# Block-sparse attention with an FFN: transposes of P into the free score columns, six early buffers for P, and more buffers for its halves

## The chip, the cores and the metric

The kernel runs on one core of a Trainium2 chip. The metric is the device time of one execution in microseconds (us), the median of several runs.

Engines are named as the profile names them: PE is TensorE's matmuls, PEld its weight loads, DVE is VectorE, ACT is ScalarE, POOL is GpSimd, SP is SyncE, which here only issues transfers. Each engine runs its own instructions in order and waits for other engines through semaphores.

## The reference

Attention over 4 batches of 8 heads, 768 positions, 64 wide, with a mask over blocks of 32: a block sees its neighbours, the first and last blocks, and three sampled ones. Behind it a layer norm, a feed-forward network (FFN) with a ReLU, 512 to 2048 to 512, and a residual.

```python
scores = scale * np.matmul(q, k.transpose(0, 1, 3, 2))
...
scores = np.where(mask, scores, -1000000000.0)
scores = scores - np.max(scores, axis=-1, keepdims=True)
attn = np.exp(scores)
attn = attn / (np.sum(attn, axis=-1, keepdims=True) + 1e-09)
x = np.matmul(attn, v)           # then (B, S, 8 * 64)
...
xn = (x - mu) / np.sqrt(var + 1e-06) * g_ln
out = x + np.maximum(xn @ w_ch1, 0.0) @ w_ch2
```

## The kernel before

Numbers that go into a matmul are split into a high and a low half in f16, and a product is the sum of three: high by high, high by low, low by high. In tile names `kh`, `kl` are the halves of k, `qh`, `ql` of q, `ph`, `pl` of P, `xh`, `xl` of the normed rows, `hh`, `hl` of the hidden layer, `w1h`, `w1l`, `w2h`, `w2l` of the weights. The weights come in a wide integer form and are unpacked on DVE (lines 514 to 564) out of the raw tiles `w1r` and `raw`.

The work is cut into 12 units of 256 rows (of one batch), each with 4 pairs of heads: 48 segments. A segment has two tiles of 128 rows by two heads: 4 slots, 192 in all. Scores are made for two slots at a time, a pair: slots 2n and 2n+1 are pair n. Each of the two slots has a score tile `ps` in PSUM, 128 partitions by 1024 floats, of which the scores fill columns 0 to 767; a PSUM bank holds 512 floats of each partition, so a score tile spans two banks. The chain for a slot is: scores on PE (L587) into `ps`; masked max on DVE (L596) from `ps` and the mask table `allow` into `p`, with the maximum in `st` (the tile `st2n` is that of pair n); the exponential on ACT (L610), in place in `p`.

After that there are two ways. The first 9 segments (EARLY, 36 slots) go through PE: P is transposed in f32, four of its six 128-column tiles into one PSUM bank and the other two into another (L625; three tiles `bank`, 512 floats each, shared with the FFN and the layer norm), ACT copies both out into `pt` (L632), PE multiplies with v (L701), spreads the sums over partitions (L726), and DVE scales (L733). The other segments make `ph` on ACT (L662) and `pl` on DVE (L666), transpose both by DMA from SP's queue (L672, L675), and multiply with v (L705, L710). The raw keys lie in two buffers `raw0`, `raw1` of 2 x 768 floats, of which the loads use the first 768.

After four segments a unit is complete; it gets its layer norm, then the FFN (L302). The first unit's FFN is placed among the scores of later segments. DVE builds the mask table in two parts: one for the first 256 rows, and one for the rest (L314 to L319), with an integer table in `w1h`'s place.

The order on every engine is made by a planner when the program is built (class `Plan`). Tasks have an engine, a cost in ns, a rank, the tasks that they follow, and resources that they take and give back: rings, whose places go round, and choices, in which the place that came free first is taken. At each step the planner takes the task that can start first by its own costs and emits its instructions. It also puts filler matmuls (ones by ones) into early gaps of PE. The numbers near the head of the function set ranks and choices: MASKAT is the rank of the second part of the mask table, EASE the slack that a task is planned with (PE below rank 44, PE above, other engines above), EXPO and EVAC shift the ranks of exponentials and copies, KDVE and QDVE say how many low halves of k and q DVE makes rather than POOL, CASTK and CASTQ how many high halves ACT casts rather than POOL's DMA. Real waits are semaphores that the framework sets from the tiles and banks that instructions touch, not from the planner's costs.

Of the kernel before, what the change touches and what calls it, by code (L numbers as in the profile page):

```python
# [10 lines left out]
F16 = mybir.dt.float16  # L11
F32 = mybir.dt.float32
# [164 lines left out]
def sparse_attention_moe(  # L177
# [12 lines left out]
    nc = tc.nc  # L190
    P = 128
    B, NPAIR, NCH, _, CH = qs.shape
    D = P // 2
    S = ks.shape[3]
# [10 lines left out]
    NQ = 4  # L205
    UPS = H * TS

    EARLY = 9
    EARLYLN = 1
    EASY, EASE = 44, (249, 2530, 951)  # L210
    PORC = ((2, 0), (2, 7), (1, 1), (2, 11), (2, 9), (1, 6), (2, 13), (2, 10), (1, 4), (2, 1), (2, 2))
# [3 lines left out]
    SPLITAT = 7.38  # L215
    VDVE = 1
    KDVE, QDVE = 3, 1
    HIDMA = ((1, 5), (2, 15), (2, 2), (1, 7), (2, 5), (2, 4))
    LEAD = 2.8
    HIGHAT, LOWAT = -0.42, -1.36  # L220
    EVAC, EXPO = -9.12, 1.22
    PLAIN = 'full'
    LOWDVE = ((2, 12), (1, 3), (2, 2), (1, 6), (1, 1), (2, 8), (2, 11), (1, 7), (2, 4), (2, 15), (2, 6), (2, 3), (1, 0), (2, 13), (2, 5))
    AVHOLD = 4
    KEEP = 40000.0
    CASTK, CASTQ = 5, 6
    MASKAT = 25.07
    KAT, VAT, QAT = 11.39, 7.48, 12.65
    AVAT = -17.05
    W1AT = (8.87, 9.4, 10.72, 12.06, 12.3, 15.45, 16.92, 18.19)  # L230
    W2AT = (10.6, 14.04, 14.21, 15.7, 17.12, 20.44, 21.31, 22.16, 23.71, 24.25, 25.32, 25.67, 25.7, 25.75, 26.19, 28.74)
# [5 lines left out]
    pp = ctx.enter_context(tc.tile_pool(name="pp", bufs=2))  # L237
# [6 lines left out]
    ps_s = ctx.enter_context(tc.tile_pool(name="ps_s", bufs=2, space=bass.MemoryType.PSUM))  # L244
# [4 lines left out]

    plan = Plan()  # L250
# [33 lines left out]
    ql_s = [const.tile([P, CH], F16, name=f"ql{i}") for i in range(NQ)]  # L284
    w1h = const.tile([P, CT, DF], F16, name="w1h")
# [54 lines left out]
    def loads_k(b, pr, rank, before):  # L340
        idx = b * NPAIR + pr
        o = SimpleNamespace()

        def raw():
# [3 lines left out]
            nc.sync.dma_start(o.kr, ks[b, pr])  # L348
# [4 lines left out]
        o.raw = plan.add("SP", 580, raw, (before,), rank, 2000, load=1120, order="k",  # L353
# [5 lines left out]
        else:  # L359
            o.high = plan.add("POOL", 560, lambda: nc.gpsimd.dma_start(o.kh, ks[b, pr]),  # L360
                              (o.raw,), rank, 2300, load=1100, order="k")
# [4 lines left out]
    def loads_q(n, rank, before):  # L366
        u, pr = segs[n].u, segs[n].pr
        o = SimpleNamespace()

        def raw():  # L370
# [4 lines left out]
            nc.sync.dma_start(o.qr, qs[u.b, pr, u.c])  # L375

        o.raw = plan.add("SP", 580, raw, (before,), rank, 2000, load=370, order="q",
# [5 lines left out]
        else:  # L383
            o.high = plan.add("POOL", 560, lambda: nc.gpsimd.dma_start(o.qh, qs[u.b, pr, u.c]),  # L384
                              (o.raw,), rank, 2300, load=400, order="q")
# [47 lines left out]
    def loads_v(b, pr, rank, before):  # L433

        o = SimpleNamespace(idx=b * NPAIR + pr, vr={}, raw=[])
        early = any(x.early for x in segs if (x.u.b, x.pr) == (b, pr))
# [11 lines left out]
        for j in range(2):  # L448
            def raw(j=j):
# [6 lines left out]
                nc.sync.dma_start(dst.rearrange("p t d -> p (t d)"), v[b, 2 * pr + j])  # L456

            take = (() if early else (("vr", (o.idx, j)),)) + ((("v", o.idx),) if j == 0 else ())
            o.last = plan.add("SP", 580, raw, (o.last,), rank, 2000, load=550, take=take, order="v")
# [8 lines left out]
    def loads_w(kind, i, before, w1done, low_tail):  # L468

        o = SimpleNamespace()  # L470
        own = (kind, i)
        if kind == 1:
# [11 lines left out]
        def load():  # L484
# [18 lines left out]
            nc.sync.dma_start(o.raw.rearrange("p e t -> p (e t)"),  # L503
# [33 lines left out]
        ld = plan.add("SP", 580, load, after if kind == 1 or i >= 10 else after + tuple(  # L537
# [29 lines left out]
        if own in HIDMA and own in PORC:  # L567
            o.high = plan.add("POOL", 560, lambda: nc.gpsimd.dma_start(o.dh, o.src), (d,), rank + HIGHAT,
                              2300, load=1500 * size)
# [20 lines left out]
    def masked_max(s):  # L590
        s.p = pp.tile([P, S], F32, tag="p", name=f"p{s.i}", bufs=4)
# [21 lines left out]
    def attention_early(seg, pair, e_done):  # L613
        r = pair[0].i
        for s in pair:
            key = (seg.i, s.h % 2)
            x4 = x2 = None
            for part, (lo, hi) in enumerate(((0, 4), (4, KT))):
# [3 lines left out]
                def turn(s=s, lo=lo, hi=hi, own=own):  # L622
                    dst = bank[plan.where("bank", own)]
# [4 lines left out]
                def out_(s=s, lo=lo, hi=hi, own=own, dve=dve, key=key):  # L628
                    if key not in pts:
                        pts[key] = ptp.tile([P, KT, CH], F32, tag="pt", name=f"pt{key[0]}_{key[1]}")  # L630
                    src = bank[plan.where("bank", own)][:, 0 : (hi - lo) * P]
# [4 lines left out]
                             take=(("bank", own),), give=(("p", s.i),) if part else ())  # L636
                take = (("pt", key),) if s.t == 0 and part == 0 else ()
                y = plan.add("DVE" if dve else "ACT", 335 if dve else (470, 300)[part], out_,
                             (x,) if part == 0 else (x, seg.first[key]) if s.t == 0 else (x,),
                             r + EVAC, 130, take=take, give=(("bank", own),))  # L640
# [4 lines left out]

    def attention(seg, pair, e_done):
        r = pair[0].i

# [7 lines left out]
        for s in pair:  # L656
            key = (seg.i, s.h % 2)

            def high(s=s):
                s.ph = pp.tile([P, S], F16, tag="ph", name=f"ph{s.i}")  # L660
# [3 lines left out]
            def low(s=s):  # L664
                s.pl = pp.tile([P, S], F16, tag="pl", name=f"pl{s.i}")
# [11 lines left out]
            h = plan.add("ACT", 830, high, (inv,), r, 120, take=(("ph", s.i, 2),))  # L677
# [449 lines left out]
```

## Time and profile before

| | |
|---|---|
| time, median of 3 runs | 794.59 us (793.11 to 795.34) |
| the profiled execution | 792.63 us, its span 790.9 us |
| instructions on PE, DVE, ACT, POOL | 7327, 1216, 935, 140 |
| costliest group of matmuls | 204.6 us, the FFN's second layer, high by high |
| masked maxima on DVE | 192, 178.1 us, 950 ns each |
| exponentials on ACT | 192, 178.4 us, 931 ns each |
| `pl` on DVE | 156, 160.1 us, 1040 ns each |

The span is the time from the first to the last instruction of one profiled execution; that execution's own time lies 1.7 us above it. Busy times are sums over an engine's instructions. A row of the timeline has an instruction's start, its length, engine, line, what it writes and reads, and in brackets the idle time before it with what ended it. A row of the waits has the waiting engine and line, what it waited for, the total, how often, and the longest.

### The profile page before, as it was taken

To read this page: it belongs to the slowest core of one execution; us is meant where nothing else is said; L and a number is where in the kernel's file an instruction comes from. 1 tells how busy PE (TensorE), PEld (TensorE's weight loads), DVE (VectorE), ACT (ScalarE), POOL (GpSimd) and SP (SyncE) were. 2 spreads that over 40 slices of the span, in tenths; PEclk is the share of its full clock that TensorE was granted. 3 is DMA by queue.
4 is the path that set the end of the run, shared out by engine and by line. 5 is a ranking of instruction groups with operands and counts; after the bars stand their busy time and mean duration, and the time that the engine had idled before them with its cause. 6 is when DMAs were issued, how large, how long until landed. Compare 5 with 4: busy or idle time off the path is not lost.

```text
span 790.9 us, 18452 instructions
## 1 busy us (share of the span) xinstructions
PE 777.9 (98%) x7327; PEld 599.3 (76%) x7327; DVE 615.4 (78%) x1216; ACT 498.3 (63%) x935; POOL 130.4 (16%) x140
## 2 busy tenths in 40 slices
PE   8999999999999999999999999999999999999998
PEld 5556677778777777777777777777777877778887
DVE  7999999979888778879877978778877878874220
ACT  6789776567676566667666667567656656652110
POOL 1343542321101002220101102120001100000000
PEclk9999999999999999999999999999999999999999
DMA  9463537998777567999667778997866755570000
GB/s 331 163 194 118 152 106 152 199 213 162 166 129 135 126 129 146 188 196 155 159 123 127 135 137 150 186 190 161 160 105 125 154 115 114 123 136 18 21 1 27
DMA packets 286694, 111.24 MB, mean 141 GB/s; under 512 B 253968, under 2 KB 278416, under 8 KB 286608
## 3 DMA queue, kind: packets, MB, share of 16 engines
q1 hardware_dynamic: 278544, 104.91, 61.2%
q0 software_dynamic: 7776, 5.05, 5.5%
q8 instruction: 57, 0.93, 0.5%
q14 instruction: 29, 0.24, 0.1%
q10 hardware_dynamic: 288, 0.10, 0.1%
HBM read 47.16 MB, written 6.29 MB: 68 GB/s over the span
## 4 chain that ended last, share of the span: by engine, by line
PE 88%; DVE 5%; ACT 3%; DMA 3%; issue 0%; ACTq 0%; DVEq 0%
PE bank L302 61%; PE ps L587 12%; PE pa L705 7%; PE pa L710 3%; PE pa L701 2%; PE bank L625 2%; DMA pt<-pl 2%; DVE p L596 1%; ACT p L610 1%; ACT pt L632 1%; DVE pl L666 1%; DVE allow L317 0%; DMA allow<-blocks 0%; PE pa L726 0%; PE bank L782 0%
## 5 line engine op out<-in xcount | busy, mean ns | idle before, releaser
L302 PE MATMUL bank<-hh,w2h 128*128 128x256 f16 x768 | 204.6, 273 | 0.0
L302 PE MATMUL bank<-hh,w2l 128*128 128x256 f16 x768 | 204.2, 273 | 0.0
L302 PE MATMUL bank<-hl,w2h 128*128 128x256 f16 x768 | 204.2, 273 | 0.0
L596 DVE CUSTOM_DVE_ANT_1 p<-ps,allow 128x768 f32<-128x768 f32 x192 | 178.1, 950 | 22.9 <-PE ps L587 22.6
L610 ACT ACTIVATE p<-p,st 128x768 f32<-128x768 f32 x192 | 178.4, 931 | 18.5 <-DVE st L596 18.2
L662 ACT ACTIVATE ph<-p,st 128x768 f16<-128x768 f32 x156 | 140.4, 927 | 59.6 <-DVE st L653 20.7
L666 DVE SCALAR_TENSOR_TENSOR pl<-p,st,ph 128x768 f16<-128x768 f32 x156 | 160.1, 1040 | 10.5 <-DMA pt<-pl 10.5
L302 PEld LDWEIGHTS <-w2h 128*128 128x128 f16 x1536 | 146.7, 98 | 27.0 <-issue 10.5
L302 PEld LDWEIGHTS <-w1h 128*128 128x128 f16 x1536 | 147.8, 98 | 25.5 <-issue 8.8
L302 PE MATMUL bank<-xh,w1h 128*128 128x256 f16 x768 | 115.4, 273 | 1.0 <-ACT pt L632 1.0
L302 PE MATMUL bank<-xh,w1l 128*128 128x256 f16 x768 | 115.4, 273 | 0.0
L302 PE MATMUL bank<-xl,w1h 128*128 128x256 f16 x768 | 115.4, 273 | 0.0
L889 DVE SCALAR_TENSOR_TENSOR hl<-bank,hh 128x512 f16<-128x512 f32 x96 | 66.1, 688 | 53.9 <-ACT hh L883 53.2
L883 ACT ACTIVATE hh<-bank 128x512 f16<-128x512 f32 x96 | 56.8, 591 | 75.3 <-PE bank L302 74.7
L302 PEld LDWEIGHTS <-w1l 128*128 128x128 f16 x768 | 73.8, 98 | 12.4 <-issue 4.1
L302 PEld LDWEIGHTS <-w2l 128*128 128x128 f16 x768 | 75.0, 98 | 9.1 <-issue 0.3
L705 PE MATMUL pa<-pt,vh 128*64 128x512 f16 x468 | 80.0, 383 | 0.9 <-DMA pt<-pl 0.9
L384 POOL DMA_DIRECT2D qh<-q x42 | 24.3, 579 | 277.7 <-PE ps L587 277.6
L587 PE MATMUL ps<-kh,qh 64*128 64x256 f16 (+1 forms) x384 | 66.0, 328 | 1.2 <-DVE st L596 1.1
L387 POOL TENSOR_TENSOR ql<-qr,qh 128x256 f16<-128x256 f32 x47 | 43.9, 935 | 139.9 <-DMA qr<-q 77.3
L587 PE MATMUL ps<-kl,qh 64*128 64x256 f16 (+1 forms) x384 | 64.4, 323 | 1.6 <-DVE kl L351 1.6
L587 PEld LDWEIGHTS <-qh 64*128 64x128 f16 x768 | 30.9, 94 | 45.8 <-issue 23.5
(110 smaller groups left out, 906.7 us busy)
## 6 DMA issues: line engine op xcount, KB each, us to landing
qr<-q SPq DMA_DIRECT2D x48, 128.0 KB, 2.8
raw<-k SPq DMA_DIRECT2D x16, 384.0 KB, 4.6
raw<-w SPq DMA_DIRECT2D x12, 512.0 KB, 3.9
vr<-v SPq DMA_DIRECT2D x32, 192.0 KB, 2.8
out<-ot SPq DMA_DIRECT2D x48, 128.0 KB, 1.9
w2l<-w SPq DMA_DIRECT2D x4, 1024.0 KB, 8.1
qh<-q POOLq DMA_DIRECT2D x42, 64.0 KB, 2.8
pt<-ph SPq DMA_TRANSPOSE x156, 2.7
```

The source lines that it names most:

```text
L302: nc.tensor.matmul(dst, w, x, start=start, stop=stop, skip_group_check=True)
L384: o.high = plan.add("POOL", 560, lambda: nc.gpsimd.dma_start(o.qh, qs[u.b, pr, u.c]), (o.raw,), rank, 2300, load=400, order="q")
L387: o.low = plan.add(e, x, lambda: (nc.vector if n < QDVE else nc.gpsimd).tensor_sub(o.ql, o.qr, o.qh), (o.raw, o.high), rank, give=(("qr", ...
L587: nc.tensor.matmul(s.ps[:, lo:hi], x[rows, s.qs], y[rows, lo:hi], start=n == 0, stop=n == len(terms) - 1)
L596: nc.vector.tensor_tensor_reduce(out=s.p.rearrange(blk, k=BLK), in0=s.ps[:, 0:S].rearrange(blk, k=BLK), in1=bias, scale=-0.125, scalar=3.0 ...
L610: nc.scalar.activation(s.p, s.p, AF.Exp, bias=s.st[:, j : j + 1], scale=-1.0, accum_out=total)
L662: nc.scalar.activation(s.ph, s.p, AF.Copy, scale=s.r)
L666: nc.vector.scalar_tensor_tensor(out=s.pl, in0=s.p, scalar=s.r, in1=s.ph, op0=ALU.mult, op1=ALU.subtract)
L705: nc.tensor.matmul(seg.pa[half[hh], 0 : 2 * CH], vo.vh[:, hh, t, :], pts[keys[hh]][:, t].rearrange("p i n -> p (i n)"), start=t == 0, stop ...
L710: nc.tensor.matmul(seg.pa[half[hh], 0:CH], vo.vl[:, hh, t, :], pts[keys[hh]][:, t, 0, :], start=False, stop=t == KT - 1, skip_group_check= ...
L883: nc.scalar.activation(u.hh[:, f : f + 2, :].rearrange("p f n -> p (f n)"), bank[plan.where("bank", own)], AF.Relu)
L889: nc.vector.scalar_tensor_tensor(out=u.hl[:, f : f + 2, :].rearrange("p f n -> p (f n)"), in0=bank[plan.where("bank", own)], scalar=0.0, i ...
```

## The change

The score tiles become two fixed tiles. The last two transposes of an early slot, and ACT's copy of them, use columns 768 to 1023 of a score tile rather than a `bank`; the planner has a choice "rest" of two places for these columns, apart from the ring "ps" of the score tiles. P gets six places for the early segments: four tiles, and two more that are the later halves' tiles, seen as f32. The halves get four places each: the two old ones and, from segment WIDEAT = 14 on, two in the second 768 floats of `raw0` and `raw1`. A helper `queue_of` can put loads on POOL's queue; with `POOLQ = ()` every one stays on SP's. A few planned costs and all numbers at the head of the function are changed; some are shown. The other numbers set the ranks of loads, weights and casts in the same way.

```diff
-    EASY, EASE = 44, (249, 2530, 951)
+    EASY, EASE = 44, (85, 2233, 956)
-    KDVE, QDVE = 3, 1
+    KDVE, QDVE = 12, 0
-    EVAC, EXPO = -9.12, 1.22
+    EVAC, EXPO = -16.38, 8.36
-    CASTK, CASTQ = 5, 6
-    MASKAT = 25.07
+    CASTK, CASTQ = 6, 16
+    MASKAT = 22.15
...
+    plan.choice("p", range(6))
+    plan.choice("rest", range(2))
+    plan.choice("ph", range(4))
+    plan.choice("pl", range(4))
...
+    score = [ps_s.tile([P, 1024], F32, tag=f"ps{i}", name=f"ps{i}") for i in range(2)]
...
+    p_s = [const.tile([P, S], F32, name=f"p{i}") for i in range(4)]
+    halves_s = [const.tile([P, 2, S], F16, name=f"p{n}") for n in "hl"]
+    p_s += [x.rearrange("p i s -> p (i s)").bitcast(F32) for x in halves_s]
...
-            s.ps = ps_s.tile([P, 1024], F32, tag="ps", name=f"ps{s.i}")
+            s.ps = score[plan.where("ps", s.i)]
...
-        s.p = pp.tile([P, S], F32, tag="p", name=f"p{s.i}", bufs=4)
+        s.p = p_s[plan.where("p", s.i)]
...
-                    dst = bank[plan.where("bank", own)]
+                    dst = score[plan.where("rest", own)][:, S:] if part else bank[
+                        plan.where("bank", own)]
...
-                    src = bank[plan.where("bank", own)][:, 0 : (hi - lo) * P]
+                    src = score[plan.where("rest", own)][:, S:] if part else bank[
+                        plan.where("bank", own)]
...
                 x = plan.add("PE", 110 * (hi - lo), turn, (e_done[s.i], x4), r, 230, mode="full",
-                             take=(("bank", own),), give=(("p", s.i),) if part else ())
+                             take=((("bank", "rest")[part], own),), give=(("p", s.i),) if part else ())
                 take = (("pt", key),) if s.t == 0 and part == 0 else ()
+                if part and seg.i < EARLY - 2:
+                    wides.append(x)
...
+    def half_of(n, place):
+
+        if place < 2:
+            return halves_s[n][:, place]
+        return raw_s[place - 2][:, S:].bitcast(F16)[:, n * S : (n + 1) * S]
...
+        late = seg.i >= WIDEAT
+        places = range(4 if late else 2)
+        done = tuple(x.low for x in wo2) if late else ()
...
-                s.ph = pp.tile([P, S], F16, tag="ph", name=f"ph{s.i}")
+                s.ph = half_of(0, plan.where("ph", s.i))
...
-            h = plan.add("ACT", 830, high, (inv,), r, 120, take=(("ph", s.i, 2),))
-            l = plan.add("DVE", 930, low, (h,), r, 100, lock=True, take=(("pl", s.i),),
+            free = tuple(wides) if seg.i == EARLY else ()
+            h = plan.add("ACT", 830, high, (inv,) + free + done, r, 120, take=(("ph", s.i, 2, places),))
+            l = plan.add("DVE", 930, low, (h,) + free, r, 100, lock=True, take=(("pl", s.i, 1, places),),
...
                 last_m = plan.add("DVE", 880, lambda s=s: masked_max(s), (sc, masks[u.c > 0], last_m),
-                                  s.i, 160, take=(("p", s.i),), give=(("ps", s.i),), order="m")
+                                  s.i, 160, give=(("ps", s.i),), order="m",
+                                  take=(("p", s.i, 1, range(6 if seg.i < EARLY - 2 else 4)),))
```

What the change moves is set by the planner. Three places of the built order follow. A row has the line, the operation, what it writes and reads with a number that only tells names apart, the size, and in brackets the semaphores that the instruction waits for: PE, DVE and Activation for those engines, DMAHW for a transfer. `p0`, `p1` and so on are slots before; after, `p0` to `p3`, `ph` and `pl` are the six places, and `ps0`, `ps1` the score tiles. The lines after are L604 for the scores, L613 for the masked max, L627 for the exponential, L643 for the transposes and L651 for their copies.

DVE from the first weight chunk (`w2h` from `w1r0`) on; before, slots 2 and 3 come next:

```order
L514 TENSOR_SCALAR w2h_126<-w1r0_162 128x1024 [waits DMAHW3_49]
L596 ISA p2_268,st2_269<-ps2_249,allow_112 128x768 [waits PE_49]
L596 ISA st2_269 128x1
L596 ISA p3_279,st2_269<-ps3_250,allow_112 128x768 [waits PE_49]
L596 ISA st2_269 128x1
L518 SCALAR_TENSOR_TENSOR w2h_126<-w1r0_162,w2h_126 128x1024 [waits DVE_49]
L514 TENSOR_SCALAR w2h_126<-w1r1_166 128x1024 [waits DMAHW4_49]
```

After, the second part of the mask table (four forms of row, L327 to L332) stands ahead of them:

```order
L531 TENSOR_SCALAR w2h_131<-w1r0_169 128x1024 [waits DMAHW3_49]
L327 TENSOR_TENSOR w1h_129<-allow_111,samp_i_112 128x288
L330 TENSOR_TENSOR allow_111<-allow_111,w1h_129 128x96 [waits DVE_49] x3
L332 TENSOR_SCALAR allow_111<-allow_111 128x96 [waits DVE_49]
L613 ISA p2_125,st2_278<-ps0_98,allow_111 128x768 [waits PE_49]
L613 ISA st2_278 128x1
L613 ISA p3_126,st2_278<-ps1_99,allow_111 128x768 [waits PE_49]
L613 ISA st2_278 128x1
L535 SCALAR_TENSOR_TENSOR w2h_131<-w1r0_169,w2h_131 128x1024
L531 TENSOR_SCALAR w2h_131<-w1r1_178 128x1024 [waits DMAHW6_49]
L613 ISA ph_127,st4_323<-ps0_98,allow_111 128x768 [waits PE_49,Activation_49]
```

The table moved from behind slot 7 to ahead of slot 2, and the masked max of slot 4, the last row, also waits for ACT, which copies out of `ps0`.

ACT at the same place, from the exponentials of the first two slots on, before:

```order
L610 ACTIVATE p0_217,nm0_227<-p0_217,st0_218 128x768 [waits DVE_49]
L610 ACTIVATE p1_222,nm0_227<-p1_222,st0_218 128x768 [waits DVE_49]
L632 COPY pt0_0_277<-bank2_103 128x4x128 [waits PE_49]
L632 COPY pt0_0_277<-bank0_101 128x2x128 [waits PE_49]
L632 COPY pt0_1_284<-bank1_102 128x4x128 [waits PE_49]
L610 ACTIVATE p2_268,nm0_227<-p2_268,st2_269 128x768 [waits DVE_49]
L632 COPY pt0_1_284<-bank2_103 128x2x128 [waits PE_49]
L610 ACTIVATE p3_279,nm0_227<-p3_279,st2_269 128x768 [waits DVE_49]
```

And after:

```order
L627 ACTIVATE p0_123,nm0_237<-p0_123,st0_233 128x768 [waits DVE_49]
L627 ACTIVATE p1_124,nm0_237<-p1_124,st0_233 128x768 [waits DVE_49]
L651 COPY pt0_0_284<-bank2_102 128x4x128 [waits PE_49]
L651 COPY pt0_0_284<-ps0_98 128x2x128 [waits DVE_49]
L651 COPY pt0_1_291<-bank0_100 128x4x128 [waits PE_49]
L627 ACTIVATE p2_125,nm0_237<-p2_125,st2_278 128x768
L651 COPY pt0_1_291<-ps1_99 128x2x128 [waits DVE_49,PE_49]
L627 ACTIVATE p3_126,nm0_237<-p3_126,st2_278 128x768
L372 CAST kh2_220<-raw0_117 128x768 [waits DMAHW7_49]
```

The rows stand in the same sequence; what moved is what the copies of the two-tile parts wait for: DVE rather than PE, which there is the masked max of the newer slot in the same score tile.

PE where the transposes of slots 8 and 9 stand, before the scores of the seventh pair (pair 6), before:

```order
L726 MATMUL pa1_513<-ident_106,nm1_335 64x128 x4
L625 MATMUL bank2_103<-ident_106,p8_465 128x128 [waits Activation_49]
L625 MATMUL bank2_103<-ident_106,p8_465 128x128 x3
L625 MATMUL bank1_102<-ident_106,p8_465 128x128 x2
L587 LDWEIGHTS qh3_155
L587 MATMUL ps12_545<-kh3_224,qh3_155 128x512 [waits DVE_49]
L587 LDWEIGHTS qh3_155
L587 MATMUL ps13_546<-kh3_224,qh3_155 128x512 [waits DVE_49]
```

And after, behind the spread of segment 1 too:

```order
L757 MATMUL pa1_498<-ident_105,nm1_346 64x128 x4
L643 MATMUL bank2_102<-ident_105,p2_125 128x128 [waits Activation_49]
L643 MATMUL bank2_102<-ident_105,p2_125 128x128 x3
L643 MATMUL ps0_98<-ident_105,p2_125 128x128 [waits DVE_49]
L643 MATMUL ps0_98<-ident_105,p2_125 128x128
L643 MATMUL bank1_101<-ident_105,p3_126 128x128 [waits Activation_49]
L643 MATMUL bank1_101<-ident_105,p3_126 128x128 x3
L643 MATMUL ps1_99<-ident_105,p3_126 128x128 [waits DVE_49]
L643 MATMUL ps1_99<-ident_105,p3_126 128x128
L604 LDWEIGHTS qh3_161
L604 MATMUL ps0_98<-kh3_229,qh3_161 128x512
```

Both slots' transposes now come ahead of the scores, and their two-tile parts wait for DVE, the masked max of pair 5 in the same score tile.

More of the change, by code (lines that the diff above doesn't have):

```diff
@@ L342, in loads_k @@
         o = SimpleNamespace()
+        qk = "k" if b else ""
         def raw():
@@ L347, in raw @@
             o.kr = raw_s[RAWS.index(plan.where("raw", ("k", idx)))][:, 0:S]
-            nc.sync.dma_start(o.kr, ks[b, pr])
+            queue_of(qk)[0].dma_start(o.kr, ks[b, pr])
         def low():
             (nc.vector if idx < KDVE else nc.gpsimd).tensor_sub(o.kl, o.kr, o.kh)
-        o.raw = plan.add("SP", 580, raw, (before,), rank, 2000, load=1120, order="k",
+        o.raw = plan.add(*queue_of(qk)[1:], raw, (before,), rank, 2000, load=1120, order="k",
                          take=(("k", idx), ("raw", ("k", idx), 2 if idx < RAWS_S else 1, RAWS)))
@@ L360, in loads_k @@
             o.high = plan.add("POOL", 560, lambda: nc.gpsimd.dma_start(o.kh, ks[b, pr]),
-                              (o.raw,), rank, 2300, load=1100, order="k")
+                              (o.raw,), rank, 2300, load=1500, order="k")
         e, x = ("DVE", 870) if idx < KDVE else ("POOL", 1640)
@@ L374, in raw @@
                 o.ql = ql_s[plan.where("q", n)]
-            nc.sync.dma_start(o.qr, qs[u.b, pr, u.c])
-        o.raw = plan.add("SP", 580, raw, (before,), rank, 2000, load=370, order="q",
+            queue_of(qk)[0].dma_start(o.qr, qs[u.b, pr, u.c])
+        o.raw = plan.add(*queue_of(qk)[1:], raw, (before,), rank, 2000, load=370, order="q",
                          take=(("q", n), ("qr", n)) if n >= RAWS_S else (("qr", n),))
@@ L384, in loads_q @@
             o.high = plan.add("POOL", 560, lambda: nc.gpsimd.dma_start(o.qh, qs[u.b, pr, u.c]),
-                              (o.raw,), rank, 2300, load=400, order="q")
+                              (o.raw,), rank, 2300, load=600, order="q")
         e, x = ("DVE", 345) if n < QDVE else ("POOL", 660)
@@ L455, in raw @@
                     dst = o.vr[j] = rawp.tile([P, KT, D], F32, tag="vr", name=f"vr{o.idx}_{j}")
-                nc.sync.dma_start(dst.rearrange("p t d -> p (t d)"), v[b, 2 * pr + j])
+                queue_of(qv)[0].dma_start(dst.rearrange("p t d -> p (t d)"), v[b, 2 * pr + j])
             take = (() if early else (("vr", (o.idx, j)),)) + ((("v", o.idx),) if j == 0 else ())
-            o.last = plan.add("SP", 580, raw, (o.last,), rank, 2000, load=550, take=take, order="v")
+            o.last = plan.add(*queue_of(qv)[1:], raw, (o.last,), rank, 2000, load=550, take=take, order="v")
             o.raw.append(o.last)
@@ L620, in attention_early, with turn @@
                 dve = part and (s.i % 4 >= XACT or s.i < XDVE)
-                def turn(s=s, lo=lo, hi=hi, own=own):
-                    dst = bank[plan.where("bank", own)]
+                def turn(s=s, lo=lo, hi=hi, own=own, part=part):
+                    dst = score[plan.where("rest", own)][:, S:] if part else bank[
+                        plan.where("bank", own)]
                     for t in range(lo, hi):
@@ L635, in attention_early @@
                 x = plan.add("PE", 110 * (hi - lo), turn, (e_done[s.i], x4), r, 230, mode="full",
-                             take=(("bank", own),), give=(("p", s.i),) if part else ())
+                             take=((("bank", "rest")[part], own),), give=(("p", s.i),) if part else ())
                 take = (("pt", key),) if s.t == 0 and part == 0 else ()
+                if part and seg.i < EARLY - 2:
+                    wides.append(x)
                 y = plan.add("DVE" if dve else "ACT", 335 if dve else (470, 300)[part], out_,
                              (x,) if part == 0 else (x, seg.first[key]) if s.t == 0 else (x,),
-                             r + EVAC, 130, take=take, give=(("bank", own),))
+                             r + EVAC, 130, take=take, give=((("bank", "rest")[part], own),))
                 if s.t == 0 and part == 0:
@@ L664, in low @@
             def low(s=s):
-                s.pl = pp.tile([P, S], F16, tag="pl", name=f"pl{s.i}")
+                s.pl = half_of(1, plan.where("pl", s.i))
                 nc.vector.scalar_tensor_tensor(out=s.pl, in0=s.p, scalar=s.r, in1=s.ph,
```

52 lines of the change are left out of this document (29 added, 23 removed).

## The prediction, made before the changed kernel ran

> **What bounds the kernel now.** I read the head of the page first, then the chain that ended last, then busy time by stage.
>
> ```profile
> span 790.9 us, 18452 instructions
> PE 777.9 (98%) x7327; PEld 599.3 (76%) x7327; DVE 615.4 (78%) x1216; ACT 498.3 (63%) x935; POOL 130.4 (16%) x140
> PE 88%; DVE 5%; ACT 3%; DMA 3%; issue 0%; ACTq 0%; DVEq 0%
> ...
> core 0: us, PE busy (x) PEld busy (x) DVE busy (x) ACT busy (x) POOL busy (x), PEclk, DMA share, GB/s
> 0.00:9.00 9.00, 6.23 (x42) 4.24 (x43) 4.50 (x12) 4.37 (x7) 2.42 (x9) 1.00 0.77 251
> 9.00:80.00 71.00, 66.14 (x561) 43.84 (x560) 67.50 (x118) 61.30 (x133) 23.87 (x18) 1.00 0.56 193
> 80.00:170.00 90.00, 88.10 (x817) 67.79 (x816) 83.03 (x170) 62.08 (x125) 34.98 (x32) 1.00 0.72 163
> 170.00:720.00 550.00, 550.00 (x5295) 423.60 (x5295) 442.39 (x885) 359.88 (x650) 69.15 (x82) 1.00 0.76 145
> 720.00:791.00 71.00, 67.44 (x620) 59.84 (x616) 17.95 (x34) 10.70 (x20) 0.00 (x0) 0.99 0.05 16
> ```
>
> TensorE (PE) carries 88% of the chain. From 170 to 720 us it is busy all 550.00 of 550.00 us at clock 1.00, so the change can gain nothing there: it leaves the matmuls as they are. What can move is 9 to 80 us, the early segments. There VectorE (DVE) is the tight engine, 67.50 of 71 us. PE shows 66.14, but with fillers and unpipelined matmuls in it. The first FFN matmul marks the end of this stage; behind it PE runs nearly dense, so a shift of that moment goes into the total one for one. The waits from 5 to 90 us, and one row for the whole run, show what the change is about:
>
> ```profile
> PEld bank L625 <- ACT pt L632: 6.8, 16, 1.1
> PE bank L625 <- ACT pt L632: 2.3, 4, 0.9
> PE bank L302 <- ACT pt L632: 1.0, 1, 1.0
> ...
> DVE w2h L514 <- DMA w1r<-w: 1.2, 1, 1.2
> DVE xT L733 <- ACT xT L730: 0.8, 1, 0.8
> DVE p L596 <- PE ps L587: 0.6, 2, 0.4
> DVE xl L850 <- ACT xh L846: 0.3, 1, 0.3
> ...
> DVE pl L666 <- DMA pt<-pl: 10.5, 12, 1.9
> ```
>
> Columns: total us, times, longest. Transposes wait for ScalarE (ACT) to empty a bank (6.8 and 2.3 us), yet PE has slack there. DVE, from 8.92 us up to the FFN's start, waits only 2.9 us (1.2 + 0.8 + 0.6 + 0.3). Whatever adds a wait on DVE here delays the FFN.
>
> **The change, part by part.** Matmuls: 7175 before, 7181 after. The six more are fillers, emitted where PE would stand idle: 0. Over all stages only the early one is left open, and in it the columns.
>
> *The shared bank.* A score tile is 1024 floats wide, two banks; the scores fill 768 columns, and the last two transposes of a slot now go to columns 768 to 1024. Those share a bank with score columns 512 to 767. The order as built shows what follows: those transposes wait for DVE's masked max of the newer pair in that tile, ACT's copy out of the tile too, and about 20 of the first 26 masked maxima wait for such a copy, as do the next scores. The planner keeps "rest" and "ps" as separate resources, so its order doesn't allow for these waits.
>
> [...]
>
> *The mask table.* The mask table for the second and third 256 rows is now built ahead of the third masked max instead of after the eighth.
>
> ```profile
> 8.92 0.94 DVE L596 CUSTOM_DVE_ANT_1 p<-ps,allow 128x768 f32<-128x768 f32 x1
> 11.94 0.69 DVE L514 TENSOR_SCALAR w2h<-w1r 128x1024 int32<-128x1024 int32 x1 [1.20 <-DMA w1r<-w]
> 12.55 0.95 DVE L596 CUSTOM_DVE_ANT_1 p<-ps,allow 128x768 f32<-128x768 f32 x1
> 13.43 0.95 DVE L596 CUSTOM_DVE_ANT_1 p<-ps,allow 128x768 f32<-128x768 f32 x1
> 14.30 1.22 DVE L518 SCALAR_TENSOR_TENSOR w2h<-w1r,w2h 128x1024 int32<-128x1024 int32 x1
> 15.44 0.69 DVE L514 TENSOR_SCALAR w2h<-w1r 128x1024 int32<-128x1024 int32 x1
> 20.34 0.95 DVE L351 TENSOR_TENSOR kl<-raw,kh 128x768 f16<-128x768 f32 x1
> 21.21 0.95 DVE L596 CUSTOM_DVE_ANT_1 p<-ps,allow 128x768 f32<-128x768 f32 x1
> 23.89 0.43 DVE L314 TENSOR_TENSOR w1h<-allow,samp_i 128x288 f32<-128x288 f32 x1
> 27.81 0.41 DVE L733 TENSOR_TENSOR xT<-pa,xT 128x256 f32<-128x256 f32 x1
> ...
> 12.55 1.35 ACT L632 COPY pt<-bank 128x512 f32<-128x512 f32 x3 [0.71 <-PE bank L625]
> 13.78 0.96 ACT L610 ACTIVATE p<-p,st 128x768 f32<-128x768 f32 x1
> 18.70 0.84 ACT L358 CAST kh<-raw 128x768 f16<-128x768 f32 x1
> ...
> 17.76 0.82 PE L587 MATMUL ps<-kh,qh 64*128 64x512 f16 x2
> 25.79 0.39 PE L587 MATMUL ps<-kh,qh 64*128 64x512 f16 x2
> 40.74 0.39 PE L587 MATMUL ps<-kh,qh 64*128 64x512 f16 x2
> 50.20 0.39 PE L587 MATMUL ps<-kh,qh 64*128 64x512 f16 x2
> 79.83 0.60 PE L302 MATMUL bank<-xh,w1h 128*128 128x256 f16 x4
> ```
>
> These are starts and lengths on DVE, ACT and PE. Successive starts give what an instruction takes of its engine: a masked max 0.88 (12.55 to 13.43), the long 1024-wide operation 1.14 (14.30 to 15.44), the short one 0.60, kl 0.87, the table 3.92 (23.89 to 27.81). So the third masked max moves from 12.55 to 11.94 + 0.60 + 3.92 = 16.5, ending at 17.3. ACT's copy of the first slot's last two tiles stands behind it (their tile's bank holds that slot's scores), and ACT works in order: about 4.2 us idle from 13.1 to 17.3, with two exponentials and the cast kh2 queued behind. In place of 18.70, that cast ends near 21.35, and kl2 on DVE waits 0.65.
>
> I walked DVE, ACT and PE on from there by the built order, each instruction with its duration from before. That is an estimate. The begin of a pair of scores moves thus: 4th, 17.76 to 24.4; 5th, 25.79 to 31.4; 8th, 40.74 to 45.2; 10th, 50.20 to 54.8. The moved table takes back part of the first shift, since its 3.92 no longer stands between the 4th and 5th. The masked maxima wait in turn, each for scores that stand behind a copy on ACT: the 7th 1.35, the 9th 1.1, the 15th 1.5, the 23rd 1.45, five smaller ones 1.35 together. With kl2's 0.65 and the DMA's 1.2, DVE waits 8.6 us in place of 2.9: **+5.7**.
>
> *DVE's work.* Counted at these lengths, DVE's instructions ahead of the 26th masked max take 63.7 us by the order after, 63.1 before: **+0.6**. From that masked max to the FFN's start the walk gives 4.0 to 4.6, against 4.98 in the trace (79.83 less 74.85, where the first row below shows the max done): **−0.7**.
>
> ```profile
> 74.85 0.08 DVE L596 DVE_READ_ACCUMULATOR2_ANT st<- 128x1 f32 x1
> 76.94 1.23 DVE L850 TENSOR_TENSOR xl<-xc,xh 128x1024 f16<-128x1024 f32 x1 [0.29 <-ACT xh L846]
> ```
>
> *What softens it.* The 68.0 us from 8.92 to 76.94 on DVE are 60.9 of instructions at the lengths above, 2.9 of waits, and 4.2 by which instructions take longer than elsewhere while POOL works beside them; POOL is busy 23.87 us there. If POOL's work falls into the 5.7 us in which DVE waits, 5.7/23.87 of these 4.2 go: **−1.0**. At best for the change nearly all 4.2 go: the walk without any lengthening starts the FFN at 82.4 (+2.5). At worst none goes, and what follows the 26th masked max keeps its 4.98: 5.7 + 0.6 = +6.3.
>
> *Behind the FFN's start.* The 1.0 that the first FFN matmuls wait for a bank goes; the remaining early transposes and V matmuls meet the same hazard. I take 0, bounds −2 and +2.
>
> *The halves' extra buffers.* They serve from segment 14 on, when PE is already dense. DVE's 10.5 us of waits for pt<-pl lie in its spare time (442.39 of 550). So 0. The two stalls of PE that DMA transposes do cause come earlier:
>
> ```profile
> 143.63 0.38 PE L705 MATMUL pa<-pt,vh 128*64 128x512 f16 x1 [0.23 <-DMA pt<-pl]
> 164.80 0.38 PE L705 MATMUL pa<-pt,vh 128*64 128x512 f16 x1 [0.42 <-DMA pt<-pl]
> ```
>
> *The rest.* Nine more kl on DVE at 0.95, mostly after the FFN's start: 8.6 us, hidden by 107 idle ones; without that cover each 0.95 would be PE's. Their POOL turns go. Ten more q casts on ACT in place of POOL's DMAs, each below kh's 0.84 (a third as wide), are hidden by 190 us idle. SP issues as many transfers as before (491); k0's load now stands behind a second q load, hidden, since DVE builds the first table until then. The helper that chooses a queue sends everything to SP still: 0. The last 71 us are the same matmuls: 0.
>
> **Sum.** 5.7 + 0.6 − 0.7 − 1.0 = +4.6 on a span of 790.9. That execution took 792.63 us, 2.0 below the median of 794.59. So 794.59 + 4.6 = **799 us** (+0.6%). A change under 0.3% (2.4 us) can't be told from none.
>
> **Rivals.**
> A, faster. The emptied columns take load off three banks: of 9.1 us of transposes waiting (6.8 + 2.3) and the FFN's 1.0, a third reaches the FFN's start, −3: 791.6. It decides if DVE's waits between 9 and 80 us stay near 2.9, because the six P buffers let ACT and PE run ahead, so that the copies are done when the masked maxima come. For it: ACT has 9.7 us to spare in that stage. Against: ACT's idle 4.2 us at 13 to 17 follows from order alone.
> B, no change. The waits come, but POOL's slowing falls by nearly all its 4.2 and the bank waits repay the rest: +2.5 − 2 = +0.5, 795.
> C, much slower. Beside the early delay, PE's tasks are planned with less slack against other engines (2530 to 2233 ns, EASE), so stalls like those at 143.63 and 164.80 (0.2 to 0.4 by the rows, some 1 with what follows) appear all along; ten of 0.6 give +6: 805.
>
> **How the numbers follow.** Slower: 0.60, of which C has 0.08 and my forecast 0.52, with its own range 795 to 803 (+2.5 to +6.3, widened by the ±2 behind the FFN's start). B 0.18. A 0.22. The range for 8 in 10 leaves out half of A at most and most of C: 790.5 to 805.
>
> **What would show it.** Right: transposes into a score tile that wait for DVE's masked max, masked maxima that wait for ACT's copies, ACT idle some 4 us before 18 us, DVE's waits near 8 us between 9 us and the FFN, whose first matmul comes at 82 to 86 us, and PE dense from 170 on. Wrong: FFN at 80 or earlier, or PE stalls behind 170 us. What would make the prediction wrong is the walk: it takes every duration as fixed, and one transfer that lands earlier or an order of waits that I misread shifts all that follows.

## The result: 0.6% slower, as forecast, and not for all the reasons given

The changed kernel takes 799.05 us (median of 11 runs, 796.11 to 801.23) against 794.36 before; the ratio is 1.0060, interval 1.0046 to 1.0074. Run again later beside other kernels it took 797.81 against 793.39, ratio 1.0062 (1.0047 to 1.0077). The forecast was 799.

The profiled execution took 801.23 us, the slowest of the 11, with a span of 799.5. That is 8.6 above the span before, so part of what this trace shows isn't in the median. Busy time by stage, columns as before:

```profile
9.00:80.00 71.00, 63.08 (x541) 42.22 (x538) 61.95 (x114) 59.48 (x129) 18.91 (x12) 1.00 0.52 190
80.00:170.00 90.00, 85.76 (x789) 65.45 (x786) 83.56 (x173) 66.79 (x136) 17.66 (x15) 1.00 0.56 138
170.00:720.00 550.00, 548.92 (x5272) 420.12 (x5272) 448.02 (x902) 360.43 (x657) 56.45 (x78) 1.00 0.80 147
```

From 170 us on PE is dense again but for about one microsecond, the end of a stall that began at 168 us (experiment 7). DVE's busy time from 9 to 80 us fell from 67.50 to 61.95. Its waits, from 8.9 us to 80 us, are these:

```profile
DVE w2h L531 <- DMA w1r<-w: 1.4, 1, 1.4
DVE p L613 <- PE ps L604: 1.3, 1, 1.3
DVE p L613 <- ACT pt L651: 1.2, 1, 1.2
DVE xT L764 <- ACT xT L761: 1.2, 2, 0.8
DVE nm L1067 <- ACT pl L627: 1.1, 1, 1.1
DVE ph L613 <- ACT pt L651: 1.1, 2, 0.8
DVE kl L365 <- ACT kh L372: 1.0, 2, 0.7
DVE w1l L581 <- ACT w1h L575: 0.5, 1, 0.5
```

They sum to 8.8 us, where 2.9 stood before. Masked maxima (lines with p or ph) do wait for ACT's copies out of a score tile, 2.3 us, but only three times; by their semaphores some 20 of them could have. Transposes into a score tile wait for DVE's masked maxima, and scores for ACT's copies, as forecast (PE, whole run):

```profile
PE ps L643 <- DVE st L613: 3.8, 6, 0.9
PE ps L604 <- ACT pt L651: 2.3, 3, 1.4
```

To place the loss, I took from the time at each landmark what PE has to do up to there by the order: every matmul at the usual spacing of its form in these traces (0.109 us for a 256-wide f16 one). What is left is PE's lost time so far, in us; the same spacings serve for all kernels, so differences count and not levels. This is a working of mine and no view of the profile, and its differences are good to about half a microsecond: the FFN itself starts 2.8 us later (82.62 against 79.83), where the table has 3.0.

| kernel | FFN starts at | lost up to there | to unit 0's second layer | to unit 1's FFN | to unit 1's second layer | to the end |
|---|---|---|---|---|---|---|
| before | 79.8 | 22.6 | 24.4 | 25.1 | 26.3 | 30.5 |
| changed | 82.6 | 25.6 | 30.0 | 30.2 | 34.8 | 39.0 |
| changed, without the extra halves' places | 82.3 | 25.3 | 29.6 | 29.9 | 30.1 | 34.3 |

Three differences carry it: 3.0 up to the FFN's start, 2.6 in the FFN's first layer, and 3.4 near 168 us. The last belongs to some executions only (experiment 7); in its place the stalls of before at 143 and 164 us are gone. Without it, 2.7 + 2.5 − 1.4 = 3.8 us, near the median's 4.7 and 4.4.

The second one could be read off directly: PE just after the FFN's start, ACT at that moment, and in a third fence the last of these casts in the kernel before.

```profile
82.62 0.39 PE L315 MATMUL bank<-xh,w1h 128*128 128x256 f16 x2
83.45 0.27 PE L315 MATMUL bank<-xh,w1h 128*128 128x256 f16 x1 [0.44 <-ACT xh L877]
84.24 0.27 PE L315 MATMUL bank<-xh,w1h 128*128 128x256 f16 x1 [0.52 <-ACT xh L877]
85.50 0.60 PE L315 MATMUL bank<-xl,w1h 128*128 128x256 f16 x4 [0.55 <-DVE xl L881]
```

```profile
82.73 0.37 ACT L651 COPY pt<-ps 128x256 f32<-128x256 f32 x1 [1.06 <-PE ps L604]
82.99 0.41 ACT L877 CAST xh<-xc 128x256 f16<-128x256 f32 x1
83.78 0.41 ACT L877 CAST xh<-xc 128x256 f16<-128x256 f32 x1
```

```profile
76.50 0.41 ACT L846 CAST xh<-xc 128x256 f16<-128x256 f32 x1
```

ACT's copy of two transposed tiles waits 1.06 us for the newer scores in the same score tile, and behind it stand the third and fourth cast of the normed rows, for which the first layer waits. Before, the fourth was begun 3.3 us ahead of the FFN (76.50, FFN at 79.83); now it is begun 1.2 us behind its start. Further on, transposes into score tiles wait for DVE and scores for ACT's copies, 0.5 and 0.4 us once each.

### The profile page after: what moved, and what is told of

It is laid out like the page before. It is cut to its first block, busy times and chain, and to the rows that moved or that the text cites. A ratio compares the mean times of both kernels' runs of the same rounds, so it can differ in the third digit from the quotient of the medians.

```text
span 799.5 us, 18496 instructions
## 1 busy us (share of the span) xinstructions
PE 780.4 (98%) x7333; PEld 600.2 (75%) x7333; DVE 615.1 (77%) x1227; ACT 502.5 (63%) x947; POOL 96.2 (12%) x114
## 4 chain that ended last, share of the span: by engine, by line
PE 86%; DVE 7%; ACT 3%; DMA 2%; issue 1%; POOL 0%; SPq 0%; DVEq 0%; ACTq 0%
PE bank L315 60%; PE ps L604 12%; PE pa L736 7%; PE pa L741 3%; PE pa L732 2%; DVE p L613 2%; ACT pt L651 1%; DMA w1r<-w 1%; ACT p L627 1%; PE bank L643 1%; DVE pl L696 1%; PE ps L643 1%; DMA pt<-pl 1%; DVE raw L539 1%; DMA raw<-k 1%
## 5 line engine op out<-in xcount | busy, mean ns | idle before, releaser
L613 DVE CUSTOM_DVE_ANT_1 p<-ps,allow 128x768 f32<-128x768 f32 x184 | 170.4, 949 | 26.1 <-PE ps L604 24.4
L627 ACT ACTIVATE p<-p,st 128x768 f32<-128x768 f32 x184 | 170.6, 929 | 14.1 <-DVE st L613 11.3
L692 ACT ACTIVATE ph<-p,st 128x768 f16<-128x768 f32 x88 | 78.7, 927 | 31.7 <-issue 21.4
L696 DVE SCALAR_TENSOR_TENSOR pl<-p,st,ph 128x768 f16<-128x768 f32 x88 | 88.8, 1025 | 6.4 <-DMA pt<-pl 4.0
L692 ACT ACTIVATE raw<-p,st 128x768 f16<-128x768 f32 x68 | 60.8, 927 | 19.6 <-issue 13.8
L604 PE MATMUL ps<-kh,qh 64*128 64x256 f16 (+1 forms) x384 | 66.4, 329 | 4.6 <-ACT pt L651 2.3
L696 DVE SCALAR_TENSOR_TENSOR raw<-p,st,raw 128x768 f16<-128x768 f32 x68 | 70.0, 1047 | 0.3
L604 PEld LDWEIGHTS <-qh 64*128 64x128 f16 x768 | 31.6, 94 | 48.7 <-issue 26.8
L936 DVE SCALAR_TENSOR_TENSOR ot<-bank,xT 128x256 f32<-128x256 f32 x48 | 20.1, 421 | 60.4 <-PE bank L315 60.3
```

The source lines that it names most:

```text
L604: nc.tensor.matmul(s.ps[:, lo:hi], x[rows, s.qs], y[rows, lo:hi], start=n == 0, stop=n == len(terms) - 1)
L613: nc.vector.tensor_tensor_reduce(out=s.p.rearrange(blk, k=BLK), in0=s.ps[:, 0:S].rearrange(blk, k=BLK), in1=bias, scale=-0.125, scalar=3.0 ...
L627: nc.scalar.activation(s.p, s.p, AF.Exp, bias=s.st[:, j : j + 1], scale=-1.0, accum_out=total)
L692: nc.scalar.activation(s.ph, s.p, AF.Copy, scale=s.r)
L696: nc.vector.scalar_tensor_tensor(out=s.pl, in0=s.p, scalar=s.r, in1=s.ph, op0=ALU.mult, op1=ALU.subtract)
L936: nc.vector.scalar_tensor_tensor(out=ot, in0=src(), scalar=1.0 / (SW1 * SW2), in1=u.xT[:, e, :], op0=ALU.mult, op1=ALU.add)
```

## Experiments

**1. The transposes back in a bank.** The numbers, six places and four halves' places of the change stay.

```diff
-                    dst = score[plan.where("rest", own)][:, S:] if part else bank[...]
+                    dst = bank[plan.where("bank", own)]
-                             take=((("bank", "rest")[part], own),), ...
+                             take=(("bank", own),), ...
```

> The changed kernel, with the last two transposes of an early slot back in a bank of their own, as before the change; all its numbers and buffers stay. If the shared bank of score tile and transposes makes the delay: no masked max waits for ACT's copies any more but two, DVE waits under 5 us from 9 us to the FFN, the FFN starts at 80 to 81 us (82.6 in the changed kernel) and the time is 795 to 797. If the new order of tasks makes it, the FFN still starts at 82 to 83 and the time stays at 798 to 800.

Measured: 799.94 us, ratio 1.0067 (1.0050 to 1.0085). The waits did as the first theory says, and the time as the second. These are its DVE waits of 0.5 us and more, 8.9 to 80 us, and two of PE's in the whole run:

```profile
DVE p L613 <- PE ps L604: 2.0, 3, 1.1
DVE xT L762 <- ACT xT L759: 0.8, 2, 0.6
DVE xc L865 <- ACT rs L860: 0.6, 1, 0.6
DVE w2h L531 <- DMA w1r<-w: 0.5, 1, 0.5
DVE w1l L581 <- ACT w1h L575: 0.5, 1, 0.5
```

```profile
PE ps L604 <- DVE st L613: 2.9, 7, 0.9
PE bank L642 <- ACT pt L649: 2.8, 5, 0.9
```

No masked max waits for a copy of ACT's, and DVE waits 4.9 us in all, with two smaller ones (0.3 and 0.2). The first layer no longer waits for xh. But PE waits for banks again, and the FFN starts at 88.2 us with one pair of scores and one slot's six transposes more ahead of it; the lost time there is 29.5, which is 3.9 more than with the columns. By an estimate most of these 3.9 us are lost to the clock. The third column from the end (PEclk) is the clock granted to TensorE, as a share of the full one:

```profile
68.00:72.00 4.00, 1.61 (x11) 0.86 (x11) 3.71 (x6) 3.51 (x8) 0.00 (x0) 0.92 0.08 14
72.00:76.00 4.00, 4.00 (x16) 2.63 (x13) 3.75 (x8) 1.09 (x3) 0.00 (x0) 0.50 0.71 248
76.00:80.00 4.00, 4.00 (x24) 2.58 (x22) 3.09 (x8) 2.42 (x6) 1.83 (x2) 0.73 0.67 193
```

PE was busy only 1.61 of 4 us from 68 to 72 us, and the granted clock was 0.50 and 0.73 behind that. The missing shares, 0.08, 0.50 and 0.27 of 4 us each, come to 3.4 us; that is the estimate. The changed kernel's profile has 1.00 in this stage, and 7 of its 11 runs have 1.000 over the whole span; the six runs here lie at 0.993 to 0.997, which is 2.4 to 5.6 us of 800, estimated in the same way. So the experiment takes the waits away and brings a loss of another kind. With the median of the six clocks, 0.996, the time without that loss would be near 797 us, an estimate, and within the range of the first theory. Whether the columns cost time this run can't tell.

**2. The numbers of before in the changed code.** Every tuned number and planned load of before, in the code of after.

```diff
-    EASY, EASE = 44, (85, 2233, 956)
+    EASY, EASE = 44, (249, 2530, 951)
-    MASKAT = 22.15
+    MASKAT = 25.07
...
```

> The changed kernel's code (columns, six places for P, four for the halves) with all the planner's numbers and loads of before. If the shared bank makes the delay: FFN from 82 us on, time 797 to 800. If the new numbers make it: FFN at 80, time 793.5 to 795.5.

Measured: 811.54 us, ratio 1.0218 (1.0192 to 1.0244), beyond both expectations: neither theory had a price for numbers that no longer fit the code.

**3. The same with the transposes in a bank**, and **4.** also without the extra halves' places (`WIDEAT = 48`), so that of the change the six places for P are left, and the rule that takes the place that came free first where places went round before.

> The changed kernel with the numbers of before and with the last two transposes in a bank: of the change only the six places for P and the four places for the halves are left. With the columns and these numbers it took 811.5 us. If the columns cost it, about 794 to 797 (the halves' extra places may cost up to 2); if the six places or the halves cost it, 800 or more.

> As the kernel with the numbers of before and the transposes in a bank, and also without the extra places for the halves: of the change only the six places for P are left. If these are neutral, 794 to 795.5, and the difference to the kernel with the extra places tells what these cost with the numbers of before: 0 by my prediction, 2 if they make the planner put products with v too early, as the stall at 168 us suggests.

Measured: 808.62 us, ratio 1.0188 (1.0172 to 1.0204), and 809.40, ratio 1.0210 (1.0196 to 1.0224). So with the old numbers the six places and that rule cost 14 us or more, as the second theory of experiment 3 says; the columns add about 3, by the ratios 0 to 5 us. Part of all three times is the clock: the runs of experiments 2 to 4 lie at 0.990 to 0.998, some 2 to 8 us of 810 by the same estimate. In experiment 3 the FFN starts at 84.8 us with only 2.6 more lost than before, and the price comes later:

```profile
PE bank L315 <- DVE hl L918: 4.1, 1, 4.1
PE bank L642 <- ACT pt L649: 2.5, 4, 1.1
PE bank L315 <- ACT xh L875: 2.5, 3, 1.7
PE bank L315 <- DVE xl L879: 2.0, 3, 0.9
```

These are PE's longest waits there. One stall of 4.1 us stands at 163 to 167 us; the others wait for later units' normed rows. Six places let more early scores and transposes go ahead of the FFN (15 pairs, 14 before). That every later task then lands at another place than its rank was chosen for is my explanation, and no run tests it.

**5. The numbers of after in the code of before**: four places for P, banks, two halves' places.

> The kernel before (four places for P, two for the halves, transposes in banks) with all the planner's numbers and loads of the changed kernel. With the six places and the numbers of before the time was 808 to 809. If numbers and places only go together, this is as far off, 802 to 812, with stalls of the FFN behind 80 us; if the new numbers are good by themselves, 793 to 796.

Measured: 799.61 us, ratio 1.0063 (1.0044 to 1.0083). Neither expectation: the time is the changed kernel's, with no shared score tile and no extra place in the code. But it isn't the same loss. The FFN starts at 73.48 us, behind 12 pairs of scores (14 in the changed kernel). In the profiled execution, the longest of the six, the clock is 0.61 from 64 to 68 us, and PE stands still for 3.26 us before 175.62, for a transfer issued at 170.43:

```profile
64.00:68.00 4.00, 4.00 (x18) 2.13 (x18) 4.00 (x8) 2.71 (x5) 0.00 (x0) 0.61 0.02 4
```

```profile
170.43 1.33 SPq L675 DMA_TRANSPOSE pt<-pl  x1
```

```profile
175.62 0.40 PE L705 MATMUL pa<-pt,vh 128*64 128x512 f16 x1 [3.26 <-DMA pt<-pl]
```

All six runs have a clock below 1.000 (0.996 to 0.999). So with the new numbers about the same time comes out with columns (the changed kernel), without them (experiment 1) and without any of the change's code (here), and it is made of different losses each time.

**6. A planner that knows the shared tile.** A score tile's place and the columns for transposes are one resource.

```diff
-    plan.choice("rest", range(2))
+    plan.choice("ps", range(2))
...
-                             take=((("bank", "rest")[part], own),), ...
+                             take=((("bank", "ps")[part], own),), ...
-                          take=(("ps", a.i), ("ps", b.i)), give=give)
+                          take=(("ps", a.i, 1, (0,)), ("ps", b.i, 1, (1,))), give=give)
```

> The changed kernel with a planner that knows the shared bank: the columns for the transposes are the same resource as the score tile's place, so that it orders them one after the other with what they cost. If the delay comes from waits that the planner did not see, it can order around them: DVE's waits fall to 4 to 6 us, FFN at 80.5 to 82, time 796 to 798. If the wait itself is the price, whatever the order: FFN at 82.5 to 84, time 799 to 801.

Measured: 819.71 us, ratio 1.0308 (1.0285 to 1.0330). The FFN starts at 90.96 us behind only 11 pairs of scores, with some 20 us more lost than in the kernel before, and the time is far beyond both expectations:

```profile
9.00:80.00 71.00, 58.20 (x439) 39.15 (x435) 63.30 (x107) 51.38 (x107) 22.45 (x14) 0.89 0.56 200
```

PE did 439 matmuls from 9 to 80 us, 541 in the changed kernel, at a granted clock of 0.89, and ACT was busy 51.38 us. With one resource the planner takes a tile out of use for scores from transpose to copy. It is inconclusive on the price of the waits themselves, since the numbers weren't chosen for it either.

**7. The extra halves' places.** Without them (`WIDEAT = 48`), and from segment 22 (`WIDEAT = 22`), and the changed kernel once more beside the latter.

> The changed kernel without the two extra places for the halves of P in the raw key buffers (WIDEAT 48: no segment uses them). By my prediction they are worth nothing: 798 to 800, PE dense from 175 us on in both. If they let DVE and ACT run ahead in a way that helps, slower, 801 or more; if they cause the stall of PE at 168 us, faster by 2 to 3 us.

> The changed kernel with the halves' extra places from segment 22 on, not 14. If the extra places cost time only by the stall at 168 us, near segment 14, this gives the time of the kernel without them, 797 to 798.5. If they do it wherever they begin, another stall of PE stands some 100 us later and the time is 798.5 to 800.

> The changed kernel once more, unchanged, beside the others. If the stall of PE at 168 us (2.4 us and slow matmuls behind it) belongs to the order of the instructions, it is there again within 0.5 us; if it came from one late transfer in one execution, it is below 1 us or gone and the time of this profiled execution is 797 to 798.5. The median should be 798 to 800.

Measured: 797.74 us without, ratio 1.0036 (1.0021 to 1.0051); 798.52 from segment 22, ratio 1.0067 (1.0052 to 1.0081); 797.81 once more, ratio 1.0062 (1.0047 to 1.0077). The first is just below what "worth nothing" gave, and the second lies between its two expectations, so neither decides. The stall in the changed kernel's profile, PE and SP's queue:

```profile
168.27 0.40 PE L736 MATMUL pa<-pt,vh 128*64 128x512 f16 x1
171.08 0.38 PE L736 MATMUL pa<-pt,vh 128*64 128x512 f16 x1 [2.40 <-DMA pt<-pl]
...
166.60 1.22 SPq L705 DMA_TRANSPOSE pt<-pl  x1
```

Its wait in the profile of the changed kernel once more, and the same place without the extra places:

```profile
PE pa L736 <- DMA pt<-pl: 3.1, 1, 3.1
```

```profile
167.96 0.41 PE L736 MATMUL pa<-pt,vh 128*64 128x512 f16 x2
...
165.27 1.21 SPq L705 DMA_TRANSPOSE pt<-pl  x1
```

The order up to this place is the same in both kernels. By it, the transposes that this product waits for are the first that read a half out of a raw key buffer. The last of them landed 4.5 us after its issue (166.60 to 171.08), where the one out of the old place took 2.7 at most (165.27 to 167.96). A place in a raw key buffer isn't needed for it, though: in experiment 5, with the two old places alone, such a transfer took 5.2 us (170.43 to 175.62). And the two profiled executions with the stall took 801.23 and 801.42 us, the longest of their kernel, and the other five runs of the second took 797.19 to 798.39: it isn't in every execution. Behind the stall the clock of the changed kernel is 0.66 from 171 to 175 us. Its four runs over 800 us are the ones with a clock under 1.000 (0.996 to 0.998); without the extra places 4 of 9 runs are under 1.000 too. What makes such a transfer late stays open; experiment 9 prices the places on one chip.

**8. The mask table in a wait, in the kernel before.** The table's second part is built right after slot 1's masked max. All other instructions keep their order on all engines.

```diff
     def masked_max(s):
...
+        if s.i == 1:
+            build_mask(TS, KT)
...
-             plan.add("DVE", 1300, lambda: build_mask(TS, KT), (), MASKAT, 100, lock=True)]
+             plan.add("DVE", 1300, lambda: None, (), MASKAT, 100, lock=True)]
```

> The kernel before, with the second part of the mask table built right after slot 1's masked max, in the 1.2 us in which DVE waits for the first weights; all other instructions keep their order on every engine. If DVE's work before the FFN sets its start, as the prediction's sum assumes, the 3.92 us that the table takes between the 8th and 9th masked max go and 0.3 come at its new place: FFN at 76.3 to 78 us, time 791 to 792.5. If another engine catches up, the FFN starts at 79 to 80 and the time stays at 794.

Measured: 792.68 us, ratio 0.9978 (0.9966 to 0.9990): 0.2% faster than the kernel before. But the FFN starts at 79.79 us, 79.83 before. DVE where the table had stood, its new place first, and POOL at the later time:

```profile
10.25 0.45 DVE L314 TENSOR_TENSOR w1h<-allow,samp_i 128x288 f32<-128x288 f32 x1
10.74 0.85 DVE L317 TENSOR_TENSOR allow<-allow,w1h 128x96 f32<-128x96 f32 x3
12.95 0.69 DVE L514 TENSOR_SCALAR w2h<-w1r 128x1024 int32<-128x1024 int32 x1 [1.12 <-DMA w1r<-w]
...
26.16 0.42 DVE L735 TENSOR_TENSOR xT<-pa,xT 128x256 f32<-128x256 f32 x1 [1.18 <-ACT xT L732]
26.50 1.58 DVE L1037 TENSOR_SCALAR nm<-nm 128x4 f32<-128x4 f32 x1
28.21 0.93 DVE L596 CUSTOM_DVE_ANT_1 p<-ps,allow 128x768 f32<-128x768 f32 x1
```

```profile
25.65 2.40 POOL L532 TENSOR_TENSOR w2h<-w2h,w1r 128x1024 int32<-128x1024 int32 x1
```

The three table operations took 0.85 us here, 3.30 in their old place. What stands there now, a tiny operation on 4 columns, took 1.58 us in place of 0.16, up to 28.08, when POOL's operation was over (25.65 + 2.40 = 28.05). In this execution the weights also landed 1.01 later (12.95, 11.94 before), and the third to eighth masked max came about as much later. With all that and a new wait of 1.18 for ACT, the 9th masked max began 0.22 us earlier (28.21, 28.43 before), and nothing of it reached the FFN. The 1.7 us that the median gains I could not place with certainty; in this trace the stall of before at 164 us is absent (lost time at unit 1's second layer 25.3, before 26.3).

**9. The same move in the changed kernel**, with and without the extra halves' places, on one chip.

> The changed kernel with the same move of the table, from ahead of the third masked max (1.49 us there) into the wait for the weights; all else keeps its order. If a delay of the third masked max is carried through to the FFN by the waits of masked maxima, copies and scores for each other: FFN 1.0 to 1.4 us earlier, time 796.5 to 798. If the later waits absorb it: no change, 798 to 799.

> The changed kernel without the extra places for the halves and with the table in the wait. Beside the kernel with the places and the same table it prices them on one chip: 0 if the stall at 168 us belongs to the profiled execution alone, 1 to 2 us faster than that kernel (795 to 796.5) if it is there in every execution.

Measured: 796.75 us, ratio 1.0032 (1.0017 to 1.0047), and 796.80, ratio 1.0026 (1.0012 to 1.0041). The extra places are worth nothing either way in the median. Beside the kernels without the move (ratios 1.0060 and 1.0036) the move took some 2 us off with the places and 1 without; the intervals overlap, so neither is certain. The FFN starts at 81.9 and 81.4 us, 0.7 and 0.9 earlier than without the move.

## Why the prediction was right, and where it was not

*The total*: +4.6 predicted, +4.7 and +4.4 measured.

*DVE's waits*: 8.6 us predicted for 9 us to the FFN, 8.8 measured. The parts differ: the masked maxima wait 3.6 us, 1.3 for scores and 2.3 for the copies themselves, where the walk had 6.75, all for scores; more falls to xT, nm and kl. So that the sum fits is luck.

*The table*: this step failed. It was priced at 3.92 us from its row before; at its new place it took 1.49 (12.78 to 14.27):

```profile
12.78 0.45 DVE L327 TENSOR_TENSOR w1h<-allow,samp_i 128x288 f32<-128x288 f32 x1
13.26 0.85 DVE L330 TENSOR_TENSOR allow<-allow,w1h 128x96 f32<-128x96 f32 x3
14.27 0.95 DVE L613 CUSTOM_DVE_ANT_1 p<-ps,allow 128x768 f32<-128x768 f32 x1
15.26 0.37 ACT L651 COPY pt<-ps 128x256 f32<-128x256 f32 x1 [2.08 <-DVE st L613]
22.21 0.39 PE L604 MATMUL ps<-kh,qh 64*128 64x512 f16 x2
```

```profile
25.01 2.35 DVE L317 TENSOR_TENSOR allow<-allow,w1h 128x96 f32<-128x96 f32 x1
```

```profile
24.82 2.42 POOL L532 TENSOR_TENSOR w2h<-w2h,w1r 128x1024 int32<-128x1024 int32 x1
```

The second and third fence are from before the change: one of the table's three operations on `allow`, which take 0.85 us together at the new place, took 2.35 alone, up to 27.36. POOL's 2.42 us ended at 27.24. I had read such lengthening as a sum over the stage (4.2 us) and not looked for it in the one row that I moved. So ACT was idle 2.08 us, not 4.2 (fourth row), and the 4th pair of scores began at 22.21 rather than 24.4. In experiment 8 an operation on 128 x 4 floats, 0.16 us in the kernel before (at 28.15), took 1.58 beside POOL's 2.40. Why operations of DVE take longer beside POOL's, and which of them, no run shows.

*The FFN's start*: +4.6 predicted, +2.8 measured. The walk's pairs were late by 2.2 at the 4th (24.4 for 22.21), 0.7 at the 10th (54.8 for 54.09) and 1.8 at the FFN. DVE's waits grew by 5.9 us and the start moved by 2.8, so the three other terms, −1.1 in the sum, come to about −3.1 by this reckoning; the table's 2.4 is about that difference, and no run measured the terms one by one.

*Behind the FFN's start*: 0 with bounds −2 and +2 predicted, +2.6 in the first layer in this trace (30.0 − 25.6 against 24.4 − 22.6), beyond the bound, and some −1.4 later (kernel without the extra places). The shared score tile enters here by way of the casts of xh, which the prediction didn't look at. One term is 1.8 too high, the other 2.6 too low: they nearly cancel, and that the total came out is luck.

*The halves' places*: 0 predicted, 0 in the medians of experiment 9, some 2 us by the ratios of experiment 7, which were not taken side by side. The stall of some 3 us in single executions wasn't foreseen.

*That DVE sets the FFN's start*: this premise doesn't hold as it was used. Experiment 8 moves the table off DVE's path in the kernel before, and the FFN doesn't move, though weights that landed 1.01 later took a part of the gain. Most of the rest came back as a wait for ACT (1.18) and as the operation beside POOL (1.42 longer).

*The cause*: the waits that the shared score tile makes are shown, place by place. The prediction lays them to a bank; that is the author's reading, and no run takes the bank apart from the tile. In the changed kernel's trace the first matmuls of the 3rd pair of scores, into columns 0 to 511, began at 15.69 us after 1.38 of waiting for ACT's copy out of columns 768 to 1023 (15.26 to 15.63), so here the wait went beyond columns 512 to 1023. That the shared tile makes the kernel slower is not shown: without it the same numbers take as long (experiment 1), and the same numbers in the old code, too (5). Nor is it refuted: both lose time to the clock (0.993 to 0.997 and 0.996 to 0.999, where 7 of the changed kernel's 11 runs have 1.000), so an equal time doesn't mean an equal cause. What is shown is that the old numbers don't carry over to the new code, 808 to 812 us. What costs the 4 us stays open; no run took the new numbers one by one, and none repeats experiment 1 with the clock kept up. Of the rivals, A (faster) and C (stalls all along) are out, and B by its time, though what B rests on is there: less slowing by POOL, as the table's 2.4 us.

## What to carry to other kernels

A planner whose numbers were chosen for one set of buffers is part of the code: a change to buffers alone, tried with the old numbers, measures the misfit too and not the buffers alone. A run that takes one loss away can bring another, so look at the granted clock (0.50 and 0.73 over 8 us of experiment 1) before an equal time is read as no effect. Before an instruction is priced from its row, look what POOL did at that moment (here one table operation took 2.35 us beside POOL, three took 0.85 elsewhere); the length may belong to the place and move to whatever stands there next. And a predicted total that comes out right is no proof of its terms: here two of them were off by 1.8 and 2.6 us in opposite directions.

## What the runs showed of the hardware

Beside POOL's 2.40 us operation (25.65 to 28.05) a DVE operation on 128 x 4 floats took 1.58 us, up to 28.08, where the kernel before has 0.16; the operation just ahead of it, xT out of pa and xT at 26.16, took 0.42, the median of its nine in the kernel before (experiment 8). In the kernel before, beside POOL's 2.42 us (24.82 to 27.24), one table operation took 2.35 us, up to 27.36; in the changed kernel's trace all three take 0.85.

After a stretch in which PE was busy 1.61 of 4 us, the granted clock was 0.50 and 0.73 in the next two stretches of 4 us, with PE busy 4.00 of 4 us in both (experiment 1); behind the stall of 2.40 us at 168 us it was 0.66 from 171 to 175 us (experiment 7).
